# Scores and values in PSUM tiles of two banks, another order of the start-up, and twelve weight loads issued by ACT

## The chip, the cores and the metric

The kernel runs on one core of a Trainium2 chip. The metric is the device time of one execution in microseconds (us), the median over several runs. The engines are named as the profile names them: PE (TensorE, matrix multiplies), PEld (its weight loads), DVE (VectorE), ACT (ScalarE), POOL (GpSimd) and SP (SyncE, which only issues DMAs). A row with SPq or ACTq is a DMA being issued by that engine.

## What is computed

Attention over keys and values that are averaged in groups of eight, then a LayerNorm and a feed-forward block with a residual. There are 8 batches, 8 heads, 576 queries of 64 numbers a head; after the averaging 72 keys remain. All inputs and the output are float32.

```python
k_p = k.reshape(B, H, Sp, 8, D).mean(axis=3)      # 576 keys become 72
v_p = v.reshape(B, H, Sp, 8, D).mean(axis=3)
scores = scale * np.matmul(q, k_p.transpose(0, 1, 3, 2))
attn = np.exp(scores - np.max(scores, axis=-1, keepdims=True))
attn = attn / (np.sum(attn, axis=-1, keepdims=True) + 1e-09)
x = np.matmul(attn, v_p)                           # heads side by side: 4608 tokens x 512
xn = (x - mu) / np.sqrt(var + 1e-06) * g_ln
out = x + np.maximum(xn @ w_ch1, 0.0) @ w_ch2      # 512 -> 2048 -> 512
```

## The kernel before

The 4608 tokens are 36 tiles of 128; four tiles are a chunk of 512 tokens, so there are 9 chunks. A batch has 576 tokens, which is four and a half tiles, so that some tiles (4, 13, ...) hold the end of one batch and the start of the next.

*One tile of attention.* `scores` multiplies the queries `q` with the averaged keys `kblk` into PSUM (L282: 4 pairs of heads, 2 x 72 = 144 columns each, two pairs to a bank), takes the maximum over each head's 72 scores on DVE (L292, `mx`) and subtracts it (L294, `e`). A tile has two halves of four heads, each in a PSUM bank of its own, so there are two reductions of 288 columns and two subtractions. `probs` takes the exponential on ACT (L303), casts it to a high and a low float16 part (`phl`, ACT L304 and L307, POOL L311 and L314), and SP transposes it by a DMA (L321, `pt`). `values` multiplies it with the averaged values `va` and `vb` (L342, L345; 65 columns a head, the last one the sum), again in two halves of four heads in a bank each; DVE adds 1e-9 to the sums (L354, `sm`), inverts them, and DVE and ACT write the tile's `x` (L358, L365). Then comes the LayerNorm: L369 to L375, three Newton steps (L384 and L387), and `z` (L391), which is cast to two float16 parts (`hl`, ACT L395, POOL L396) and transposed by a DMA (L400, `zT`).

*The feed-forward block.* A product of floats is made of three float16 products (high by high, high by low, low by high). `ffn_in` runs 12 matmuls for 128 hidden units and a group of tokens (L419) and evicts the result with relu into a `ring` tile (ACT L427, DVE L428). `ffn_out` runs 24 matmuls for a tile and half of the hidden units (L448) and adds the result onto `x` (DVE L458). The ring has four tiles of 1 MB. For chunk 0 the columns are halved: columns 0 to 255 are tiles 0 and 1, columns 256 to 511 tiles 2 and 3.

*The weights.* `w1` and `w2` come as eight blocks of 1 MB each. `load_raw` starts the DMA of a block, `convert` turns it into float32 and finds its maxima (ACT L163 and L175, DVE L166 and L167), `max_w1` and `max_w2` find a common scale of half a matrix, and `split_w` makes the two float16 parts (ACT L138, DVE L139). The tile pool `raw` has two buffers; four blocks go to the ring, which is empty at the start.

*PSUM* has eight banks: two for `ps_s` (scores), two for `ps_x` (values) and four for `ps_f` (feed-forward).

*The order.* The string START gives, by hand, the order in which the pieces of the start-up are written: R.m.b loads block b of matrix m, C.m.b converts it, M finds a scale, S splits; A.t is scores and probabilities of tile t, B.t its values and LayerNorm; I.c.q.h is a quarter q of the hidden units of chunk c for column half h, O.c.h the output matmuls. LD is the first loads, K0 and V0 batch 0's averages, HK and HV those of later batches. Each engine runs its instructions in an order that a scheduler makes out of it; SP's queue holds the loads and transposes.

Of the kernel before, what the change touches and what calls it, by code (L numbers as in the profile page):

```python
# [17 lines left out]
P = 128  # L18
# [29 lines left out]
LD K0 R.1.0 V0 A.0 B.0 C.1.0 R.1.1 R.1.2 A.1 C.1.1 R.1.3 C.1.3 A.2 B.1 HK.1.0 C.1.2 B.2 A.3 B.3 M1.0  # L48
S.1.0 S.1.1 HK.1.1 S.1.2 S.1.3 I.0.0.1 HV.1.0 HV.1.1 A.4 I.0.1.1 R.2.0 R.2.1 I.0.1.0 I.0.0.0 A.5 B.4
B.5 A.6 R.2.2 C.2.0 R.2.3 B.6 C.2.2 C.2.1 A.7 R.1.4 C.2.3 C.1.4 B.7 M2.0 S.2.0 S.2.1 R.1.5 S.2.2  # L50
S.2.3 O.0.0 I.1.1 C.1.5 R.1.6 I.1.0 O.1.0 C.1.6 R.1.7 C.1.7 M1.1 S.1.4 S.1.5 S.1.6 S.1.7 R.2.4 R.2.5
I.0.2 R.2.6 R.2.7 HK.2.0 C.2.6 C.2.4 I.0.3 C.2.5 C.2.7 HK.2.1 HV.2.0 M2.1 S.2.4 S.2.5 A.8 S.2.6 A.9
B.8 S.2.7 HV.2.1 B.9 A.10 I.1.2 A.11 B.10 B.11 I.1.3 O.1.1 HV.3.0 O.0.1 HK.3.0 HV.3.1 HK.3.1
# [6 lines left out]
def attn_ffn_kernel(ctx: ExitStack, tc: tile.TileContext, qT, kT, v, g, w1, w2, out):  # L60
# [10 lines left out]
    ps_s = ctx.enter_context(tc.tile_pool(name="ps_s", bufs=2, space=PSUM))  # L71
    ps_x = ctx.enter_context(tc.tile_pool(name="ps_x", bufs=2, space=PSUM))
# [76 lines left out]
    def load_raw(mat, b):  # L149

        raw = ring_tile() if mat == 1 and b < NKT else raw_tile()
        raws[mat, b] = raw = raw.rearrange("p a f c -> p (a f c)").bitcast(I32)
        queue = nc.sync
        queue.dma_start(out=raw, in_=(w1, w2)[mat - 1][b].bitcast(I32))
# [117 lines left out]
    def scores(t):  # L272
# [3 lines left out]
        pss = []  # L276
        for half in range(2):
            ps = ps_s.tile([P, 512], F32, name="ps_s")
            for i in range(2):
                p = 2 * half + i  # L280
                for r, b in segments(t):
                    nc.tensor.matmul(  # L282
                        ps[r, i * 2 * KV : (i + 1) * 2 * KV],
                        lhsT=q[:, p, r],
                        rhs=kblk[b % NKB][:, p, :],
                        start=True,
                        stop=True,
                    )
            pss.append(ps[:, : 4 * KV].rearrange("p (h k) -> p h k", k=KV))
        heads = [slice(0, 4), slice(4, 8)]  # L290
        for sc, hs in zip(pss, heads):
            nc.vector.tensor_reduce(out=mx[:, hs], in_=sc, axis=AX.X, op=ALU.max)  # L292
        for sc, hs in zip(pss, heads):
# [285 lines left out]
```

## Time and profile before

| | |
|---|---|
| median of 3 runs | 913.95 us (913.83 to 914.32) |
| the profiled execution | 915.27 us; its span 913.2 us |
| PE busy | 832.8 us, 91% of the span |
| DVE busy | 440.3 us, 48% |
| ACT busy | 266.2 us, 29% |
| POOL busy | 265.1 us, 29% |
| PE's clock, mean | 0.991 of full speed |
| first 159.56 us | the start-up: tiles 0 to 7 of the attention, and of chunk 0 half of the hidden units |

A row of the timeline is: start, duration, engine, line, operation, output<-input by the program's names, shape, how often, and in brackets the idle time before it and what ended it. A row of the groups is: line, engine, operation, count | busy us, mean ns of one | idle time before, and what ended most of it. A row of the waits is: engine, tile and line <- what it waited for: us in total, times, the longest. A row of the chain is: start, us, what, and it shows the work that ended last, followed back from the last instruction. A row of stretches has for each engine the busy time and in brackets the instructions, then PE's granted clock, the DMA engines' busy share and GB/s.

### The profile page before, as it was taken

How to read it: one execution, taken by the hardware profiler on the slowest of the kernel's cores; microseconds unless marked ns; L12 is line 12 of the kernel's file. 1: busy time of each engine (PE TensorE's matmuls, PEld its weight loads, DVE VectorE, ACT ScalarE, POOL GpSimd, SP SyncE). 2: the span in 40 equal slices, each digit the busy share in tenths (PEclk: the TensorE clock that was granted, in tenths of full speed). 3: DMA queues.
4: the chain of work that ended last, by engine and by line, in shares of the span. 5: the costliest groups of instructions: out<-in, count | busy, mean ns of one | idle time of the engine just before them, and what ended most of it. 6: DMA issues, size and time to landing. Idle time of an engine off the chain costs nothing.

```text
span 913.2 us, 12100 instructions
## 1 busy us (share of the span) xinstructions
PE 832.8 (91%) x4524; PEld 418.7 (46%) x4524; DVE 440.3 (48%) x1130; ACT 266.2 (29%) x513; POOL 265.1 (29%) x414
## 2 busy tenths in 40 slices
PE   2243986999999999999999999999999999999998
PEld 1232833444444444445445544544454445444443
DVE  7797698225555445246424552554254335432121
ACT  2765563204421213132313221232223123211020
POOL 5575984005611551046101540131012001200000
PEclk9999979999999999999999999999999999999999
DMA  8999884102244322344222542232222321310001
GB/s 291 281 219 254 295 221 84 32 8 79 59 93 119 91 71 47 75 102 122 55 80 47 132 67 77 47 91 62 65 58 55 63 58 35 61 44 24 1 1 46
DMA packets 137290, 84.82 MB, mean 93 GB/s; under 512 B 116112, under 2 KB 117264, under 8 KB 135184
## 3 DMA queue, kind: packets, MB, share of 16 engines
q1 hardware_dynamic: 135696, 82.86, 35.7%
q10 hardware_dynamic: 1536, 1.20, 0.5%
q8 instruction: 35, 0.57, 0.3%
q14 instruction: 23, 0.19, 0.1%
HBM read 45.09 MB, written 9.44 MB: 60 GB/s over the span
## 4 chain that ended last, share of the span: by engine, by line
PE 82%; DMA 6%; DVE 5%; POOL 3%; issue 1%; ACT 1%; SPq 1%; ACTq 0%; POOLq 0%; DVEq 0%
PE ps_f L419 39%; PE ps_f L448 39%; PE ps_s L282 3%; DMA kr<-in_kT_dram 1%; DMA vr<-in_v_dram 1%; POOL vr L229 1%; DMA zT<-hl 1%; DMA ring<-in_w_dram 1%; PE ps_x L342 1%; DVE a L384 1%; PE ps_x L345 1%; DMA raw<-in_w_dram 1%; DMA raw<-in_v_dram 1%; DVE w L167 1%; DVE raw L166 1%
## 5 line engine op out<-in xcount | busy, mean ns | idle before, releaser
L419 PE MATMUL ps_f<-zT,w 128*128 128x512 f16 (+1 forms) x1824 | 386.3, 371 | 8.8 <-DMA zT<-hl 7.9
L448 PE MATMUL ps_f<-w,ring 128*128 128x512 f16 x1728 | 382.3, 381 | 3.4 <-DVE w L139 3.0
L419 PEld LDWEIGHTS <-w 128*128 128x128 f16 x1824 | 178.1, 99 | 198.6 <-DMA zT<-hl 7.2
L448 PEld LDWEIGHTS <-ring 128*128 128x128 f16 x1728 | 168.9, 98 | 206.1 <-issue 8.5
L428 DVE SCALAR_TENSOR_TENSOR ring<-ps_f,ring 128x512 f16<-128x512 f32 (+1 forms) x152 | 99.7, 660 | 147.2 <-ACT ring L427 144.7
L427 ACT ACTIVATE ring<-ps_f 128x512 f16<-128x512 f32 (+1 forms) x152 | 86.4, 574 | 253.4 <-PE ps_f L419 228.1
L458 DVE SCALAR_TENSOR_TENSOR x<-ps_f,c_out,x 128x512 f32<-128x512 f32 x72 | 53.9, 748 | 206.9 <-PE ps_f L448 202.5
L311 POOL TENSOR_TENSOR phl<-e,phl 128x512 f16<-128x512 f32 x36 | 43.7, 1214 | 275.2 <-ACT phl L304 260.0
L282 PE MATMUL ps_s<-kblk,q 128*128 128x144 f32 (+1 forms) x320 | 55.3, 339 | 33.5 <-DMA q<-in_qT_dram 10.7
L396 POOL TENSOR_TENSOR hl<-z,hl 128x512 f16<-128x512 f32 x36 | 42.2, 1171 | 116.0 <-ACT hl L395 110.3
L303 ACT ACTIVATE e<-e 128x576 f32<-128x576 f32 x36 | 24.6, 682 | 163.0 <-DVE e L294 138.7
L282 PEld LDWEIGHTS ps_s<-kblk,q 128*128 128x128 f32 (+1 forms) x320 | 47.6, 214 | 41.8 <-issue 25.3
L365 ACT ACTIVATE x<-ps_x,rs 128x64 f32<-128x64 f32 x144 | 33.4, 314 | 81.3 <-DVE rs L356 60.6
L229 POOL TENSOR_TENSOR vr<-vr 72x256 f32<-72x256 f32 x56 | 47.7, 858 | 24.8 <-DMA vr<-in_v_dram 24.4
L342 PE MATMUL ps_x<-va,pt 128*128 128x65 f16 (+1 forms) x320 | 28.0, 202 | 24.5 <-DVE x L358 12.6
L219 POOL TENSOR_TENSOR kblk<-kr 64x72 f32<-64x72 f32 x58 | 26.2, 452 | 72.0 <-PE ps_s L282 68.9
L304 ACT CAST phl<-e 128x1024 f16<-128x1024 f32 x36 | 37.5, 1042 | 4.6 <-DMA pt<-phl 4.0
L342 PEld LDWEIGHTS <-pt 128*128 128x128 f16 (+1 forms) x320 | 24.0, 105 | 31.2 <-issue 12.5
L395 ACT CAST hl<-z 128x512 f16<-128x512 f32 x36 | 22.2, 617 | 49.7 <-DVE z L391 49.0
L384 DVE SCALAR_TENSOR_TENSOR a<-y,ve 128x1 f32<-128x1 f32 x108 | 33.5, 310 | 2.9
L292 DVE TENSOR_REDUCE mx<-ps_s 128x4 f32<-128x288 f32 x72 | 31.6, 448 | 3.6 <-PE ps_s L282 3.3
L294 DVE TENSOR_TENSOR e<-ps_s,mx 128x288 f32<-128x288 f32 x72 | 30.7, 448 | 5.1 <-POOL phl L314 5.0
(81 smaller groups left out, 469.9 us busy)
## 6 DMA issues: line engine op xcount, KB each, us to landing
raw<-in_w_dram SPq DMA_DIRECT2D x12, 1024.0 KB
q<-in_qT_dram SPq DMA_DIRECT2D x36, 256.0 KB
out_dram<-x SPq DMA_DIRECT2D x36, 256.0 KB
kr<-in_kT_dram SPq DMA_DIRECT2D x30, 288.0 KB
vr<-in_v_dram SPq DMA_DIRECT2D x56, 144.0 KB
ring<-in_w_dram SPq DMA_DIRECT2D x4, 1024.0 KB
raw<-in_v_dram SPq DMA_DIRECT2D x8, 144.0 KB
va<-vh ACTq DMA_DIRECT2D x16, 65.0 KB
```

The source lines that it names most:

```text
L229: eng.tensor_add(out=vr[:, 0:4, :], in0=vr[:, 0:4, :], in1=vr[:, 4:8, :])
L282: nc.tensor.matmul(ps[r, i * 2 * KV : (i + 1) * 2 * KV], lhsT=q[:, p, r], rhs=kblk[b % NKB][:, p, :], start=True, stop=True,)
L304: nc.scalar.copy(out=ph[:, :, :, 0:KA], in_=e[:, :, 0:KA].unsqueeze(1).broadcast_to([P, 2, H, KA]))
L311: nc.gpsimd.tensor_tensor(out=ph[:, 0, :, KA:P], in0=e[:, :, 0:KA], in1=ph[:, 0, :, 0:KA], op=ALU.subtract)
L342: nc.tensor.matmul(px[r, i, :], lhsT=pt[:, h, r], rhs=VA[b][:, h, :], start=True, stop=False)
L384: nc.vector.scalar_tensor_tensor(out=a, in0=y, scalar=ve, in1=y, op0=ALU.mult, op1=ALU.mult)
L396: nc.gpsimd.tensor_tensor(out=zhl[:, 1, :], in0=z, in1=zhl[:, 0, :], op=ALU.subtract)
L419: nc.tensor.matmul(ps, lhsT=w[:, part, fs], rhs=zT[:, kz, cols], start=(n == 0), stop=(n == 3 * NKT - 1),)
L427: nc.scalar.activation(out=h[:, 0, i, cols], in_=ps, func=AF.Relu)
L428: nc.vector.scalar_tensor_tensor(out=h[:, 1, i, cols], in0=ps, scalar=0.0, in1=h[:, 0, i, cols], op0=ALU.max, op1=ALU.subtract,)
L448: nc.tensor.matmul(ps, lhsT=h[:, part, i, cols], rhs=w[:, wp, j], start=(n == 0), stop=(n == 3 * NFT // 2 - 1),)
L458: nc.vector.scalar_tensor_tensor(out=x, in0=ps, scalar=c_out[:, half : half + 1], in1=x, op0=ALU.mult, op1=ALU.add)
```

## The change

It has three parts. The pools `ps_s` and `ps_x` have one buffer each in place of two, and a tile of them spans two banks: a tile's eight heads lie in one PSUM tile, the maxima are one reduction of 576 columns, the subtraction is one instruction, and so is the addition to the sums. The matmuls keep their number and shapes; those of `values` now run over all eight heads for each batch in turn. START is another order. And `load_raw` issues only the first four blocks of `w1` on SP's queue, the other twelve on ACT's; the first two blocks go to `raw` tiles and two to the ring, and the first values go to the ring. Of START only the first line is shown.

```diff
-LD K0 R.1.0 V0 A.0 B.0 C.1.0 R.1.1 R.1.2 A.1 C.1.1 R.1.3 C.1.3 A.2 B.1 HK.1.0 C.1.2 B.2 A.3 B.3 M1.0
...
+LD K0 R.1.0 V0 A.0 R.1.1 B.0 A.1 R.1.2 C.1.2 C.1.0 B.1 A.2 R.1.3 C.1.1 HK.1.0 C.1.3 A.3 R.2.0 M1.0
...
-    ps_s = ctx.enter_context(tc.tile_pool(name="ps_s", bufs=2, space=PSUM))
-    ps_x = ctx.enter_context(tc.tile_pool(name="ps_x", bufs=2, space=PSUM))
+    ps_s = ctx.enter_context(tc.tile_pool(name="ps_s", bufs=1, space=PSUM))
+    ps_x = ctx.enter_context(tc.tile_pool(name="ps_x", bufs=1, space=PSUM))
...
-        raw = ring_tile() if mat == 1 and b < NKT else raw_tile()
+        early = mat == 1 and b < NKT
+        raw = ring_tile() if early and b >= 2 else raw_tile()
         raws[mat, b] = raw = raw.rearrange("p a f c -> p (a f c)").bitcast(I32)
-        queue = nc.sync
+        queue = nc.sync if early else nc.scalar
         queue.dma_start(out=raw, in_=(w1, w2)[mat - 1][b].bitcast(I32))
...
-        for half in range(2):
-            ps = ps_s.tile([P, 512], F32, name="ps_s")
...
+        ps = ps_s.tile([P, 2, 512], F32, name="ps_s")
+        for p in range(NPAIR):
+            for r, b in segments(t):
+                nc.tensor.matmul(
+                    ps[r, p // 2, p % 2 * 2 * KV : (p % 2 + 1) * 2 * KV],
...
-        for sc, hs in zip(pss, heads):
-            nc.vector.tensor_reduce(out=mx[:, hs], in_=sc, axis=AX.X, op=ALU.max)
-        for sc, hs in zip(pss, heads):
-            nc.vector.tensor_tensor(
-                out=e[:, hs, :],
...
+        nc.vector.tensor_reduce(out=mx, in_=sc, axis=AX.X, op=ALU.max)
+        nc.vector.tensor_tensor(
+            out=e.rearrange("p (a h) k -> p a h k", a=2),
+            in0=sc,
+            in1=mx.unsqueeze(3).broadcast_to([P, 2, 4, KV]),
+            op=ALU.subtract,
+        )
...
-            px = ps_x.tile([P, H // 2, D + 1], F32, name="ps_x")
...
+        ps = ps_x.tile([P, 2, 512], F32, name="ps_x")
+        px = ps[:, :, : H // 2 * (D + 1)].rearrange("p a (h d) -> p a h d", d=D + 1)
+        for r, b in segs:
+            for h in range(H):
+                o = px[r, h // 4, h % 4]
...
-        for half, px in enumerate(pxs):
-            hs = slice(half * 4, half * 4 + 4)
-            nc.vector.tensor_scalar_add(out=sm[:, hs], in0=px[:, :, D], scalar1=1e-9)
+        nc.vector.tensor_scalar_add(
+            out=sm.rearrange("p (a h) -> p a h", a=2), in0=px[:, :, :, D], scalar1=1e-9
+        )
...
-            raw_tile().rearrange("p a f c -> p (a f c)").bitcast(F32)[:KV].rearrange(
+            ring_tile().rearrange("p a f c -> p (a f c)").bitcast(F32)[:KV].rearrange(
```

What it moves in an engine's queue is shown at three places. The lines of the new kernel are lower or higher by a few: L164 and L176 are the old L163 and L175, L155 the old L154, L253 and L254 the old L252 and L253, L289 and L290 the old L292 and L294, L299 the old L303, L300 and L303 the old L304 and L307, L372 and L375 the old L384 and L387, L379 the old L391, L383 the old L395, L415 and L416 the old L427 and L428. A number behind a name is that of the tile. DMAHW names, with a number, the completion semaphore of a DMA that the instruction waits for.

ACT's queue in the first third of the start-up, before; `va` and `vb` are the values of batch 0.

```order
L163 ACTIVATE w1_88<-ring_278 128x1024 [waits DMAHW1_49]
L303 ACTIVATE e_284<-e_284 128x576 [waits DVE_49,Pool_49]
L138 ACTIVATE vh_187<-vp_152,sv_186 72x8x64 [waits DVE_49]
L304 CAST phl1_105<-e_284 128x16x64 [waits Activation_49]
L307 CAST phl1_105<-e_284 128x8x16
L163 ACTIVATE w1_88<-ring_280 128x1024 [waits DMAHW2_49]
L175 ACTIVATE ring_278,wm1_95<-w1_88 128x1024 [waits DVE_49]
L252 DMA va_188<-vh_187 64x520 [waits DMAHW6_49,Activation_49]
L253 DMA vb_189<-vh_187 8x520 [waits DMAHW7_49]
```

The same place after; raw_406 and raw_435 are the first two blocks of `w2`, and e_273 is tile 1.

```order
L164 ACTIVATE w1_88<-raw_219 128x1024 [waits DMAHW1_49]
L155 DMA raw_406<-in_w2_dram 128x2048 [waits DMAHW4_49,Activation_49]
L299 ACTIVATE e_273<-e_273 128x576 [waits DVE_49]
L300 CAST phl1_105<-e_273 128x16x64 [waits Activation_49]
L303 CAST phl1_105<-e_273 128x8x16
L176 ACTIVATE raw_219,wm1_95<-w1_88 128x1024 [waits DVE_49]
L138 ACTIVATE vh_187<-vp_152,sv_186 72x8x64 [waits DVE_49]
L164 ACTIVATE w1_88<-ring_289 128x1024 [waits DMAHW2_49]
L155 DMA raw_435<-in_w2_dram 128x2048 [waits DMAHW5_49,Activation_49]
L253 DMA va_188<-vh_187 64x520 [waits DMAHW6_49,Activation_49]
L254 DMA vb_189<-vh_187 8x520 [waits DMAHW7_49]
```

Two loads now stand between the conversions, one ahead of tile 1's exponential and one ahead of `va`, each with a wait for an earlier DMA's semaphore of its own.

ACT's queue where batch 1's `va` and `vb` are issued, before.

```order
L427 ACTIVATE ring_559<-ps_f_605 128x256 [waits PE_49]
L138 ACTIVATE vh_671<-vp_622,sv_670 72x8x64 [waits DMAHW0_49,DVE_49]
L252 DMA va_672<-vh_671 64x520 [waits DMAHW7_49,Activation_49]
L253 DMA vb_673<-vh_671 8x520 [waits DMAHW0_49]
L252 DMA va_672<-vh_671 64x520 [waits DMAHW2_49]
L253 DMA vb_673<-vh_671 8x520 [waits DMAHW4_49]
L427 ACTIVATE ring_710<-ps_f_711 128x256 [waits PE_49]
```

The same place after; raw_1083 is a block of `w1`, z_503 and z_552 are tiles 2 and 3, and e_1035 is tile 7.

```order
L155 DMA raw_1083<-in_w1_dram 128x2048 [waits DMAHW2_49,Activation_49]
L299 ACTIVATE e_1035<-e_1035 128x576 [waits DVE_49]
L138 ACTIVATE vh_588<-vp_441,sv_587 72x8x64 [waits DVE_49]
L253 DMA va_589<-vh_588 64x520 [waits Activation_49]
L383 CAST hl_505<-z_503 128x512 [waits DMAHW7_49,DVE_49]
L254 DMA vb_590<-vh_588 8x520
L253 DMA va_589<-vh_588 64x520 [waits DMAHW0_49]
L254 DMA vb_590<-vh_588 8x520 [waits DMAHW2_49]
L383 CAST hl_554<-z_552 128x512 [waits DVE_49]
L415 ACTIVATE ring_652<-ps_f_653 128x256 [waits PE_49]
L415 ACTIVATE ring_652<-ps_f_668 128x256 [waits PE_49]
```

The `va` and `vb` stood between evictions of chunk 0 (L427), and the tiles' casts were done; now they stand ahead of the first eviction, and the casts of tiles 2 and 3 stand between and behind them.

DVE's queue before, around tile 3's `z` (z_518).

```order
L387 SCALAR_TENSOR_TENSOR y_508<-a_509,y_508 128x1
L384 SCALAR_TENSOR_TENSOR a_509<-y_508,ve_507 128x1
L387 SCALAR_TENSOR_TENSOR y_508<-a_509,y_508 128x1
L391 TENSOR_SCALAR z_518<-x_475,mv2_504,y_508 128x512
L294 TENSOR_TENSOR e_1128<-ps_s_1130,mx_1129 128x288
L294 TENSOR_TENSOR e_1128<-ps_s_1133,mx_1129 128x288
L166 TENSOR_SCALAR raw_1147<-raw_1147 128x1024
```

DVE's queue after, from tile 7's subtraction (e_1035) to tile 2's `z` (z_503).

```order
L290 TENSOR_TENSOR e_1035<-ps_s_1037,mx_1036 128x576
L372 SCALAR_TENSOR_TENSOR a_494<-y_493,ve_492 128x1
L363 TENSOR_SCALAR y_542<-ve_541 128x1
L133 TENSOR_REDUCE allmax_581<-ps_f_584 128x1
L167 TENSOR_SCALAR raw_1077<-raw_1077 128x1024
L375 SCALAR_TENSOR_TENSOR y_493<-a_494,y_493 128x1
L372 SCALAR_TENSOR_TENSOR a_543<-y_542,ve_541 128x1
L111 TENSOR_SCALAR sv_587<-allmax_581 128x1
L250 TENSOR_SCALAR cv_594<-allmax_581 128x1
L168 SCALAR_TENSOR_TENSOR w1_88<-w1_88,raw_1077 128x1024
L379 TENSOR_SCALAR z_503<-x_462,mv2_489,y_493 128x512
```

Tile 7's subtraction, one instruction of 576 columns, stood behind tile 3's `z` (there as e_1128 in two halves) and stands now ahead of the `z` of tiles 2 and 3.

58 lines of the change are left out of this document (18 added, 40 removed).

## The prediction

> **What bounds the kernel now.** I read the stretches first, cut where PE's state changes: the fourth score tile's LayerNorm, the first FFN matmul, the first output matmul, the first matmul of chunk 1.
>
> ```profile
> core 0: us, PE busy (x) PEld busy (x) DVE busy (x) ACT busy (x) POOL busy (x), PEclk, DMA share, GB/s
> 0.00:79.26 79.26, 25.84 (x154) 20.28 (x154) 65.65 (x169) 41.48 (x70) 50.16 (x83) 1.00 0.95 256
> 79.26:154.15 74.89, 57.43 (x394) 37.41 (x394) 58.88 (x130) 40.14 (x74) 54.98 (x76) 0.93 0.81 227
> 120.58:159.56 38.98, 29.92 (x161) 14.65 (x161) 35.68 (x86) 16.99 (x32) 25.34 (x32) 0.85 0.59 135
> 159.56:913.20 753.64, 747.30 (x3968) 359.08 (x3968) 312.44 (x821) 182.03 (x365) 157.72 (x254) 1.00 0.26 63
> ```
>
> From 159.56 on PE is busy 747.30 of 753.64 us, and the change leaves its matmuls as they are; whatever DVE, ACT or POOL save there is covered by PE, and what remains is 6.3 us of gaps. Before 159.56 PE has much idle time, DVE little: 65.65 of 79.26 and 58.88 of 74.89. So the change can pay, or cost, in the start-up, and the question is when PE starts chunk 1. Next, PE's timeline at the ends of its gaps:
>
> ```profile
> 88.81 8.02 PE L419 MATMUL ps_f<-zT,w 128*128 128x256 f16 x48 [6.82 <-DMA zT<-hl]
> 159.56 22.29 PE L419 MATMUL ps_f<-zT,w 128*128 128x512 f16 x96 [1.04 <-DMA zT<-hl]
> 204.87 1.32 PE L282 MATMUL ps_s<-kblk,q 128*64 128x144 f32 x16 [1.21 <-issue]
> 218.99 10.52 PE L419 MATMUL ps_f<-zT,w 128*128 128x512 f16 x48 [0.77 <-DVE ring L428]
> ```
>
> Both starts of the FFN end on a transpose zT. The chain of waits says what stands ahead of each:
>
> ```profile
> 50.98 7.85 DMA raw<-in_w_dram
> 58.86 2.27 DVE raw L166
> 78.71 0.55 DVE z L391
> 82.96 5.80 DMA zT<-hl
> 129.98 0.68 DVE mv L235
> 153.60 0.55 DVE z L391
> 156.05 3.37 DMA zT<-hl
> ```
>
> In the chain DVE's own work runs with few breaks from 58.83, where the weight block lands, to tile 3's z (79.26), and from about 130 to tile 7's z (154.15); chunk 1 then starts 5.4 us later. Ahead of 58.83 it is a load. I therefore count DVE's queue up to these two places, and ask what interrupts it.
>
> **The change part by part.** *Merged PSUM tiles.* The rows of the old shapes, grouped by form over the first 165 us, and one pair in place:
>
> ```profile
> 81.83 0.82 DVE L292 TENSOR_REDUCE mx<-ps_s 128x4 f32<-128x288 f32 x2
> L428 DVE SCALAR_TENSOR_TENSOR ring<-ps_f,ring 128x256 f16<-128x256 f32 x16 | 6.4, 419 | 6.4 <-ACT ring L427 6.2
> L428 DVE SCALAR_TENSOR_TENSOR ring<-ps_f,ring 128x512 f16<-128x512 f32 x1 | 0.7, 691 | 3.6 <-ACT ring L427 3.6
> L354 DVE TENSOR_SCALAR sm<-ps_x 128x4 f32<-128x4 f32 x18 | 2.3, 148 | 0.6 <-PE ps_x L345 0.6
> ```
>
> No 576-wide score operation exists before. From 256 to 512 elements the PSUM-reading L428 grows by 272 ns, 1.06 ns an element; 576 would be 0.691 + 64 x 1.06 = 0.76 us, an estimate. Two halves back to back take 0.82, so each merged operation saves 0.06; its bounds are 0.69 (the 512-wide one) and 0.82 (no gain). Of the two sm additions one goes: 0.15 a tile. After the start-up all of it lies under PE.
>
> *One buffer instead of two.* PE may now write a tile's scores only when DVE has subtracted the last tile's.
>
> ```profile
> PE ps_s L282 <- DVE e L294: 2.9, 2, 1.7
> PE ps_x L342 <- DVE x L358: 12.6, 4, 4.8
> ```
>
> PE waited 2.9 us in two cases for the scores' buffers and 12.6 in four for the values' in 0 to 165, with two half tiles to spare. In the new order the FFN's first 68 matmuls stand in PE's queue behind the scores of tile 8, and these wait for DVE's subtraction of tile 7's: that subtraction is the new gate, the place that tile 3's z had. It is counted below. Elsewhere PE has idle time in the start-up, and I take nothing: between 0 and 4.8, the longest single wait.
>
> *The order.* Chunk 0's FFN begins with columns 0 to 255, which need tiles 0 and 1, where before it began with 256 to 511 (tiles 2 and 3). So tile 2's and 3's LayerNorm tails leave the stretch ahead of the gate and come behind it; two more weight conversions come ahead. DVE's rows in question:
>
> ```profile
> L167 DVE SCALAR_TENSOR_TENSOR w<-w,raw 128x1024 int32<-128x1024 int32 x12 | 16.9, 1405 | 2.4 <-ACT w L163 2.2
> L166 DVE TENSOR_SCALAR raw<-raw 128x1024 int32<-128x1024 int32 x12 | 10.5, 876 | 4.1 <-DMA raw<-in_w_dram 4.1
> L384 DVE SCALAR_TENSOR_TENSOR a<-y,ve 128x1 f32<-128x1 f32 x24 | 13.2, 550 | 0.4
> L387 DVE SCALAR_TENSOR_TENSOR y<-a,y 128x1 f32<-128x1 f32 x24 | 4.9, 204 | 0.3
> L391 DVE TENSOR_SCALAR z<-x,mv,y 128x512 f32<-128x512 f32 x8 | 5.4, 676 | 0.3
> L458 DVE SCALAR_TENSOR_TENSOR x<-ps_f,c_out,x 128x512 f32<-128x512 f32 x4 | 2.9, 730 | 0.0
> ```
>
> Ahead of the gate, counted in both programs: conversions 8 to 10, +2 x (0.876 + 1.405) = +4.56; Newton steps 12 to 8, -4 x (0.550 + 0.204) = -3.02; z 4 to 2, -2 x 0.676 = -1.35; scores 15 pairs to 16 merged, 16 x 0.76 - 15 x 0.82 = -0.14; four sm, -0.59. Sum -0.5, so the gate falls at 79.26 - 0.5 = 78.8 if nothing else moves. From the gate to tile 7's z: conversions 8 to 6, -4.56; Newton steps 12 to 16 and z 4 to 6, +4.37; one output eviction fewer, -0.73; scores 5 pairs to 4 merged, 4 x 0.76 - 5 x 0.82 = -1.06; four sm, -0.59. Sum -2.6: DVE has 58.88 - 2.6 = 56.3 us of work.
>
> What matters more is DVE's idle time in that stretch, 74.89 - 58.88 = 16.0:
>
> ```profile
> DVE ring L428 <- ACT ring L427: 6.2, 4, 2.5
> DVE raw L166 <- DMA raw<-in_w_dram: 3.1, 3, 1.5
> DVE w L167 <- ACT w L163: 1.7, 4, 0.5
> DVE e L294 <- POOL phl L314: 1.7, 1, 1.7
> ```
>
> Before, DVE had little but conversions to do while the first FFN matmuls waited 6.82 us for zT, and then waited for evictions. Now the FFN can start right at the gate, because the zT it needs was begun 24 DVE instructions earlier, and the z of tiles 2 and 3 stand between the evictions. Of 16.0 I let the loads' 3.1 and POOL's 1.7 go, and half of the 6.2; 8.1 is left. It may be as low as 3 (little but ACT's 1.7 and scraps stay) or stay at 16. PE's own work there is no bound: 57.43 us from about 81 would be done by 139.
>
> *Loads issued by ACT.* Twelve 1 MB loads leave SP's queue. What they did there, and what ACT's own DMAs did to ACT:
>
> ```profile
> 50.98 0.90 SPq L154 DMA_DIRECT2D raw<-in_w_dram  x2
> 51.99 9.39 SPq L321 DMA_TRANSPOSE pt<-phl  x1
> 159.92 1.76 SPq L321 DMA_TRANSPOSE pt<-phl  x1
> 32.68 1.12 ACT L163 ACTIVATE w<-ring 128x1024 f32<-128x1024 f32 x1 [4.27 <-DMA vr<-in_v_dram]
> 101.09 0.94 ACT L427 ACTIVATE ring<-ps_f 128x256 f16<-128x256 f32 x3 [3.01 <-DMA vb<-vh]
> 71.23 0.42 SPq L154 DMA_DIRECT2D raw<-in_w_dram  x1
> 79.45 1.16 ACT L163 ACTIVATE w<-raw 128x1024 f32<-128x1024 f32 x1 [2.89 <-DMA raw<-in_w_dram]
> ```
>
> A load takes its issuer about 0.45 us: 12 x 0.45 = 5.4 us leave SP and come to ACT, which is busy 41.48 of 79.26 us and has room. But each DMA, of either queue, uses one of eight completion semaphores in turn, and its issuer waits until the DMA eight before it has landed. SP had nothing to do behind such a wait but more DMAs; behind ACT's load of the first block of w2 stands an exponential, and behind batch 1's va and vb stand a cast hl and the first FFN evictions. Before, such a wait held ACT 4.27 us (va, vb of batch 0) and 3.01 (batch 1). Two new stalls come ahead of the gate, before the exponentials of tiles 1 and 2; each lies between 0 and 4.27, and part of it takes the place of the old 4.27, since the same queue reaches va and vb later. I take 2.5 in all, from 0 to 5.
>
> The Trainium skill, page "DMA: Bandwidth & Descriptors", section "Anatomy of one DMA — SWDGE (gpsimd) path", says that DMA engines do not wait on semaphores and that any such wait is on the sequencer which issues. By that rule the trace agrees: ACT's 4.27 us stood at its own DMAs, with nothing of ACT running.
>
> *Sum.* Gate 78.8 + 2.5 = 81.3; + 56.3 + 8.1 = 145.7 for tile 7's z; + 5.4 = 151.1 for chunk 1 against 159.56: -8.5. Behind it, the maxima of w1's second half stand ahead of chunk 1's output matmuls in the new order, so the 1.21 at 204.87 should go: -1.2 (0 to -2.0 with the 0.77). Total -9.7. The profiled execution, 913.2 of span and 2.07 around it, is 915.27, 1.3 above the median 913.95; from the median the forecast is 904.2, said as 904.
>
> **Rivals.** *Slower: ACT as issuer.* In the new program vb of batch 1 waits for the landing of a 1 MB load issued just before it. The rows at 71.23 and 79.45 show such a landing: 8.2 us from issue to use. For that time ACT would hold the cast for tile 3 and four evictions, PE would fill its four ps_f banks and stop, and DVE would wait for ACT as in its 6.2 us row. If this 8.2 falls on the path whole, the stalls ahead of the gate reach 5 (+2.5), and one later load holds ACT for 3.01, it gives 904.2 + 13.7 = 918. It decides once the stalls beyond my 2.5 pass 11.6 us. For it speaks that ACT's rows show such stalls in every batch; against it that ACT is idle half the stretch (40.14 of 74.89) and DVE has 56 us of its own to go on with. 0.21.
>
> *No change: the DMA engines bound the start.* Their share is 0.95 up to 79.26 and 0.81 after, and the chain passes 7.85 us of a weight load at 50.98. The bytes are the same. If all landings keep their time, the gate moves by little and the new order gains only what PE loses later: 913.95 - 1.2 = 912.8. Against it speaks that the share falls to 0.59 from 120.58 on, while DVE is busy 35.68 of 38.98 there: the end of the start-up is DVE's. 0.13.
>
> The Trainium skill, same page, section "Issuing engines are not separate DMA queues", holds that DMAs of several issuers run on the same engines and that a second issuer saves only the sequencer's time. By that rule moving the loads is worth nothing on this path, and the time would be this rival's. The trace does not settle it: a transpose behind two loads took 9.39 us and alone 1.76, which is what shared engines and a shared queue would both give.
>
> *More: transposes freed.* If pt's 9.39 came from standing behind SP's own weight loads, it becomes about 1.76 and the values of two tiles come 7.6 us earlier, ahead of the gate: 904.2 - 7.6 = 897. It needs DVE to have work ready then; its 13.6 idle us before 79.26 are the most that can go. 0.16.
>
> **How the numbers follow.** The forecast (899 to 911) has 0.50. About 0.2%, 1.8 us, is what a measurement can tell from none. Faster is forecast and freed transposes, 0.66; same 0.13; slower 0.21. Lower end: idle 3 (-5.1), no stall (-2.5), gaps -0.8 and part of the freed transposes: 893. Upper end: idle 16 (+7.9) and stalls 5 (+2.5) give 914.6; the slower rival's lower half reaches 917, with some 0.15 left out in all.
>
> **What would show it.** Right: chunk 1's first 96-matmul block starts near 151; the first FFN matmul near 82, right behind the scores of tile 8; DVE idle near 8 us between; no gap at 205; PE full after. Wrong: ACT idle before L299 or L383 for more than 3 us behind its own DMA rows; DVE's wait for ACT's evictions above 6.2; transposes pt still 9 us long with no load on SP's queue (then the engines are shared and the load's queue meant nothing); new waits of scores or values for DVE in 160 to 913, where I count none.

## The result, and the profile after

The changed kernel is slower: 927.76 us in the median of 20 executions (916.05 to 949.05), against 914.69 for the kernel before (912.03 to 917.07, 20 executions). The ratio of comparable executions is 1.0095, 95% interval 1.0071 to 1.0118. It leaves out executions over 1.5% above the kernel's fastest, and since this kernel alone spreads over 33 us, that cuts into its own spread; in a second series the median was 931.03 (922.64 to 938.09), ratio 1.0142 [1.0106, 1.0177]. Spread is the first finding: 5 us before, 33 after. Both profiles of the changed kernel (934.01 and 935.26 us) come from executions slower than its median, so that a typical one may lose less at the places shown.

Forecast were 904 us, a range of 893 to 917, and 0.21 for slower. Stretches of the second profile of the changed kernel (span 933.5), in the columns of the prediction; the last row is the kernel before:

```profile
core 0: us, PE busy (x) PEld busy (x) DVE busy (x) ACT busy (x) POOL busy (x), PEclk, DMA share, GB/s
0.00:80.00 80.00, 22.48 (x130) 17.57 (x130) 57.61 (x113) 38.99 (x62) 49.08 (x82) 1.00 0.96 243
80.00:160.00 80.00, 41.96 (x330) 31.99 (x331) 43.73 (x121) 35.58 (x70) 32.75 (x47) 0.89 1.11 182
200.00:930.00 730.00, 729.29 (x3891) 351.68 (x3889) 312.25 (x739) 174.97 (x356) 152.50 (x250) 1.00 0.25 63
```

```profile
80.00:160.00 80.00, 59.85 (x404) 39.24 (x404) 61.58 (x140) 42.13 (x78) 57.54 (x79) 0.91 0.77 214
```

From 200 us on PE is full, as before. The loss is in the start-up, and there every engine works less than before: DVE 43.73 of 80 us in the second stretch, against 61.58. Only the DMA engines are busier (a share of 1.11 against 0.77; it adds up the times of single packets), and they move less (182 GB/s against 214). PE's timeline, the chain of waits and a row of SP's queue of the same execution:

```profile
105.27 5.84 PE L407 MATMUL ps_f<-zT,w 128*128 128x256 f16 x48
133.01 5.09 PE L407 MATMUL ps_f<-zT,w 128*128 128x256 f16 x28 [12.96 <-DMA zT<-hl]
183.11 20.89 PE L407 MATMUL ps_f<-zT,w 128*128 128x512 f16 x96 [0.20 <-DMA zT<-hl]
```

```profile
24.25 22.11 DMA pt<-phl
83.39 20.96 DMA raw<-in_w_dram
115.95 25.51 DMA pt<-phl
```

```profile
115.95 21.25 SPq L317 DMA_TRANSPOSE pt<-phl  x1
```

The first FFN matmul comes at 105.27 (before: 88.81) and chunk 1 at 183.11 (before: 159.56). Three DMAs of 20 to 26 us stand on the chain, two transposes and a weight load; before the change the longest DMA on the chain took 11.07. SP was busy issuing the last transpose for 21.25 us, and its next DMA went out at 137.29. The longest one before:

```profile
20.86 11.07 DMA vr<-in_v_dram
```

In the first profile of the changed kernel (934.01 us) they are nearly the same ones, and a whole row of engines waits for the last:

```profile
25.78 19.00 DMA pt<-phl
82.12 16.93 DMA raw<-in_w_dram
111.77 26.55 DMA pt<-phl
```

```profile
138.34 1.04 ACT L300 CAST phl<-e 128x1024 f16<-128x1024 f32 x1 [17.10 <-DMA pt<-phl]
139.90 0.42 DVE L416 SCALAR_TENSOR_TENSOR ring<-ps_f,ring 128x256 f16<-128x256 f32 x1 [16.17 <-ACT ring L415]
140.38 5.53 PE L407 MATMUL ps_f<-zT,w 128*128 128x256 f16 x26 [14.57 <-DVE ring L416]
```

ACT stands at its cast into `phl`, whose last reader, the transpose, has not landed; the FFN's evictions are behind that cast in ACT's queue, DVE waits for ACT, and PE for DVE. In the second profile the weights are as late: in the first 200 us DVE waits 32.1 us for blocks of `raw` to land (before: 4.1).

### The profile page after: what moved, and what is told of

Same layout as the page of the kernel before. It is cut to its first block, busy times and chain, and to the rows that moved or that the text cites. A ratio compares the mean times of both kernels' runs of the same rounds, so it can differ in the third digit from the quotient of the medians.

```text
span 932.2 us, 11952 instructions
## 1 busy us (share of the span) xinstructions
PE 831.9 (89%) x4524; PEld 420.6 (45%) x4524; DVE 438.6 (47%) x1022; ACT 263.6 (28%) x513; POOL 259.9 (28%) x414
## 4 chain that ended last, share of the span: by engine, by line
PE 78%; DMA 11%; DVE 5%; POOL 2%; ACT 1%; issue 1%; SPq 0%; ACTq 0%; POOLq 0%
PE ps_f L407 37%; PE ps_f L436 36%; DMA pt<-phl 5%; PE ps_s L280 3%; DMA raw<-in_w_dram 2%; DMA kr<-in_kT_dram 2%; PE ps_x L336 1%; PE ps_x L337 1%; DVE w L168 1%; DMA ring<-in_v_dram 1%; DVE a L372 1%; DVE w L139 1%; POOL kr L216 1%; POOL phl L307 0%; DVE y L375 0%
## 5 line engine op out<-in xcount | busy, mean ns | idle before, releaser
L407 PE MATMUL ps_f<-zT,w 128*128 128x512 f16 (+1 forms) x1824 | 390.4, 374 | 21.6 <-DVE ring L416 15.6
L407 PEld LDWEIGHTS <-w 128*128 128x128 f16 x1824 | 180.3, 100 | 213.5 <-issue 21.6
L416 DVE SCALAR_TENSOR_TENSOR ring<-ps_f,ring 128x512 f16<-128x512 f32 (+1 forms) x152 | 99.7, 659 | 157.5 <-ACT ring L415 156.3
L415 ACT ACTIVATE ring<-ps_f 128x512 f16<-128x512 f32 (+1 forms) x152 | 86.7, 574 | 259.2 <-PE ps_f L407 241.4
L307 POOL TENSOR_TENSOR phl<-e,phl 128x512 f16<-128x512 f32 x36 | 42.5, 1180 | 287.5 <-ACT phl L300 273.9
L384 POOL TENSOR_TENSOR hl<-z,hl 128x512 f16<-128x512 f32 x36 | 42.7, 1186 | 115.8 <-ACT hl L383 113.8
L299 ACT ACTIVATE e<-e 128x576 f32<-128x576 f32 x36 | 24.6, 682 | 171.9 <-DVE e L290 158.4
L230 POOL TENSOR_TENSOR vr<-vr 72x256 f32<-72x256 f32 x56 | 43.2, 775 | 23.8 <-DMA vr<-in_v_dram 22.1
L300 ACT CAST phl<-e 128x1024 f16<-128x1024 f32 x36 | 37.5, 1041 | 26.2 <-DMA pt<-phl 25.6
L383 ACT CAST hl<-z 128x512 f16<-128x512 f32 x36 | 22.2, 617 | 65.7 <-DVE z L379 57.2
L232 POOL TENSOR_TENSOR vp<-vr 72x64 f32<-72x64 f32 x56 | 20.3, 373 | 59.1 <-DVE vb L139 58.8
L357 DVE BATCH_NORM_STATS2 st<-x 128x6 f32<-128x512 f32 x36 | 24.8, 690 | 23.1 <-ACT x L353 23.0
L372 DVE SCALAR_TENSOR_TENSOR a<-y,ve 128x1 f32<-128x1 f32 x108 | 31.8, 295 | 2.8
```

The costliest lines, as they stand in the source:

```text
L230: eng.tensor_add(out=vr[:, 0:4, :], in0=vr[:, 0:4, :], in1=vr[:, 4:8, :])
L300: nc.scalar.copy(out=ph[:, :, :, 0:KA], in_=e[:, :, 0:KA].unsqueeze(1).broadcast_to([P, 2, H, KA]))
L307: nc.gpsimd.tensor_tensor(out=ph[:, 0, :, KA:P], in0=e[:, :, 0:KA], in1=ph[:, 0, :, 0:KA], op=ALU.subtract)
L372: nc.vector.scalar_tensor_tensor(out=a, in0=y, scalar=ve, in1=y, op0=ALU.mult, op1=ALU.mult)
L384: nc.gpsimd.tensor_tensor(out=zhl[:, 1, :], in0=z, in1=zhl[:, 0, :], op=ALU.subtract)
L407: nc.tensor.matmul(ps, lhsT=w[:, part, fs], rhs=zT[:, kz, cols], start=(n == 0), stop=(n == 3 * NKT - 1),)
```

## The experiments

Theory A: transposes on SP's queue and 1 MB loads on ACT's meet in the DMA engines, and both get slow. Theory B, the slower rival of the prediction: ACT is held at its loads. C: the order. D: the single PSUM buffers. All times are medians, with the lowest and highest execution. The runs were made in four series; the kernel before has medians of 914.37 to 915.47 in them, so that a difference of 1 us between two series says nothing.

**The changed kernel again.** No edit.

> The changed kernel once more, for a second profile and beside the others on one chip. Every theory: median near 926, runs spread over more than 15 us, since what differs from run to run would be the timing of DMAs against each other. In the profile, transposes (pt, zT) that meet weight loads of ACT's queue land late (20 us and more) in this execution too, but perhaps others of them than in the first profile.

931.03 us (922.64 to 938.09), 5 above the expected 926; the chain above is this one. The wide spread and the late transposes came, and they are nearly the same transposes as in the first profile.

**The loads back on SP.**

```diff
-        queue = nc.sync if early else nc.scalar
+        queue = nc.sync
```

> The changed kernel with all sixteen weight loads on SP's queue; order and PSUM tiles as changed. Theory A (a transpose on one queue beside weight loads on another is slowed down by them): the time falls to 905 to 915 and the spread to some 5 us, no transpose lands later than 12 us after its issue. Theory B (ACT is held at its loads): the same fall, but the transposes stay as long as before the change, 9 to 13 us. Theory C (the new order is what costs): stays above 920. Theory D (single PSUM buffers): stays above 920.

906.58 us (905.14 to 908.39), ratio 0.9909 [0.9888, 0.9931]: 24.5 us less than the same kernel with ACT's queue in the same series (21.2 less than its first 20 executions), and a spread of 3. C and D fall as the cause of the loss. The longest transpose on the chain takes 9.02 us, within A's 12. The profile, at the places of the prediction:

```profile
24.69 9.02 DMA pt<-phl
```

```profile
83.68 8.13 PE L407 MATMUL ps_f<-zT,w 128*128 128x256 f16 x48
142.99 0.21 PE L336 MATMUL ps_x<-va,pt 128*128 128x65 f16 x1 [7.23 <-DVE z L379]
154.41 22.41 PE L407 MATMUL ps_f<-zT,w 128*128 128x512 f16 x96 [0.80 <-DMA zT<-hl]
```

The same 20 us in both kernels, loads on ACT first, loads on SP second:

```profile
84.00:104.00 20.00, 2.11 (x20) 1.87 (x21) 6.04 (x20) 4.29 (x9) 2.81 (x3) 1.00 1.08 115
```

```profile
84.00:104.00 20.00, 20.00 (x170) 16.87 (x169) 15.89 (x33) 13.26 (x27) 14.81 (x23) 1.00 1.02 282
```

The engines' share is over 1 in both; with two queues they move 115 GB/s, with one 282. The two stretches hold different DMAs (transposes and weights in the first; also q, k and v in the second), but packets of the same size differ too: one of a transpose (256 bytes) takes 97 ns on average in the first and 28 in the second, one of a weight load (8 KB) 716 and 361. At the times that the quick packets need (18 ns and 309), the packets of the first stretch would fill about a third of it, an estimate from these traces.

Counted over the first 200 us of each profile, as the packets of the trace have it (a load's packets are 8 KB, 8128 bytes with the slices and in the mirror below, partly 4 KB in the halves):

| kernel | us | transposes' packets: mean ns | those over 100 ns | loads' packets over 2 us |
|---|---|---|---|---|
| before | 915 | 25 | 169 | 1 |
| loads on SP | 907 | 24 | 233 | 0 |
| changed, first profile | 928 | 37 | 1167 | 55 |
| changed, second profile | 931 | 38 | 1171 | 60 |
| ACT's loads on the old order | 921 | 23 | 210 | 1 |
| slices | 912 | 22 | 161 | 0 |
| halves | 914 | 34 | 1500 | 3 |
| mirror | 922 | 26 | 437 | 8 |

The lower rows belong to runs that follow. The slow packets of the transposes do not go with the time. The loads' packets of over 2 us, up to 10, are many only in the changed kernel's two profiles of this table, and there they lie around the chain's three long DMAs (in the second profile 18, 26 and 16 of the 60).

**PSUM tiles alone**, on the old order with the old queue (the diff's hunks for `ps_s`, `ps_x`, `scores` and `values`).

> The kernel before with PSUM tiles of two banks, one buffer each, as the only change. Theories A, B, C: within 2 us of before, at best 1 us faster from the shorter DVE work in the start-up. Theory D: 3 us or more slower, with PE waiting for L290 or L346 in the start-up.

916.20 us (913.66 to 918.17), ratio 1.0014 [1.0000, 1.0027]. A cost of about 1 us, by the interval 2.5 at most: not D at 3 us, and no gain.

**The order alone** (START, the first blocks' places; loads on SP, old PSUM tiles).

> The kernel before with the new order and the new places of the first loads, all loads on SP, PSUM tiles as before. My sum gave the order itself about -8 us: theories A and B 903 to 914. Theory C: above 920.

902.07 us (901.24 to 902.61), ratio 0.9858 [0.9840, 0.9877]: 13 us faster, and 1 below the expected range.

```profile
80.14 7.67 PE L420 MATMUL ps_f<-zT,w 128*128 128x256 f16 x48
151.73 21.51 PE L420 MATMUL ps_f<-zT,w 128*128 128x512 f16 x96 [0.51 <-DMA zT<-hl]
```

7.8 us come ahead of chunk 1 (159.56 to 151.73) and 5.9 behind it: 899.5 - 151.73 = 747.8 against 753.64. Of the 5.9, 3.6 are work of PE that now stands ahead of chunk 1 (743.75 us busy behind it against 747.30), and 2.3 are gaps.

**ACT's loads alone**, on the old order and PSUM tiles.

```diff
-        queue = nc.sync
+        queue = nc.sync if mat == 1 and b < NKT else nc.scalar
```

> The kernel before with its twelve later weight loads issued by ACT, as the only change (old order, old PSUM tiles). On the changed order this queue cost 24.5 us (931.0 against 906.6). Theory A (transposes on one queue and 1 MB loads on another slow each other down) and theory B (ACT is held at its loads) both: 10 to 30 us slower than before, 925 to 945, with a spread of 10 us or more. Theory A's mark: a transpose that lands over 15 us after its issue. If it stays within 3 us of before, the cost belongs to the new order and the queue together.

920.94 us (919.37 to 924.73), ratio 1.0070 [1.0052, 1.0088]: slower by 6, less than either theory had. On the old order the same move costs a quarter of the 24.5, so that most of that belongs to the queue and the new order together. The profile shows no long transpose here (23 ns a packet), so A's mark is missing. It shows a load at the head of ACT's queue that waits, with the first exponential behind it:

```profile
22.18 1.28 ACT L303 ACT_TABLE_LOAD   x1 [22.18 <-DMA ring<-in_w_dram]
```

The exponential starts at 23.47 in place of 18.13. But the first transposes, which come after it, are issued at 28.17 (before: 28.21), so this wait is not shown to cost anything. Where the 6 us come from stays open.

**Small DMAs on ACT in the loads' place.** At each late load, which SP issues, ACT issues 64 bytes to a small tile.

```diff
-        queue = nc.sync if early else nc.scalar
+        queue = nc.sync
...
+        if not early:
+            nudge = wk2.tile([4, NKT], F32, name="nudge")
+            nc.scalar.dma_start(out=nudge, in_=g[0:4, :])
```

> The changed kernel with all weight loads on SP, as in the run before this one that did 906.6; at each place where ACT would issue a load it issues a DMA of 64 bytes to a small tile instead. ACT keeps its waits for completion semaphores and its issue time; the bulk is on one queue. Theory A: 905 to 910. Theory B: 920 or more.

916.78 us (915.02 to 921.36). The test was badly made: the small DMAs depend on nothing, so all twelve stand at the head of ACT's queue, and ACT does nothing until 13.43 us. It shows what twelve idle DMAs ahead of the work cost, not theory B at the loads' places.

**Slices on ACT.** SP issues the late blocks but for the last 64 bytes of each row, which ACT issues into the same tile.

```diff
-        queue = nc.sync if early else nc.scalar
-        queue.dma_start(out=raw, in_=(w1, w2)[mat - 1][b].bitcast(I32))
+        block = (w1, w2)[mat - 1][b].bitcast(I32)
+        n = block.shape[-1] if early else block.shape[-1] - 16
+        nc.sync.dma_start(out=raw[:, :n], in_=block[:, :n])
+        if not early:
+            nc.scalar.dma_start(out=raw[:, n:], in_=block[:, n:])
```

> Loads on SP as in the run that did 906.6, but the last 64 bytes of each row of the twelve later blocks are issued by ACT as a DMA of their own (8 KB in all for a block). They go to the same tile as the block, so ACT issues them at the place, and with the waits, that the changed kernel's loads had; the nudges of the earlier run could all go to the head of ACT's queue and told nothing of this. Theory B (ACT is held at its loads): 920 or more. Theory A (the bulk on a second queue): 905 to 912. In between, say 915, both matter in about equal parts.

912.49 us (911.17 to 914.86): 5.9 more than with the loads on SP alone, and just above A's 905 to 912. I count it as B's share, with all that twelve more DMAs and another order of the scheduler's bring. The wait at batch 1's `va` and `vb`, for which I had feared 8.2 us, took 5:

```profile
94.16 0.94 ACT L418 ACTIVATE ring<-ps_f 128x256 f16<-128x256 f32 x3 [5.01 <-DMA va<-vh]
```

**The mirror: bulk on ACT, slices on SP** (n = 16 in the diff above). Both queues have as many DMAs as with the slices, only the bytes change sides; the scheduler moves some instructions between the two.

> The mirror of the slices kernel: SP issues the first 64 bytes of each row of the twelve blocks, ACT the rest. Both queues have the same number of DMAs as in the slices kernel; only the bytes change sides. Theory A: 925 to 937, spread 10 us or more, transposes that take 20 us. Theory B: 911 to 915.

922.31 us (920.05 to 925.14): 9.8 more than the slices, nearer to A's range than to B's but under it. A's other signs did not come: the spread is 5, and the longest transpose takes SP 11.3 us to issue. SP's queue and PE's timeline; the row behind them is the slices':

```profile
24.08 15.90 SPq L320 DMA_TRANSPOSE pt<-phl  x2
166.08 23.44 PE L410 MATMUL ps_f<-zT,w 128*128 128x512 f16 x96 [4.94 <-DMA zT<-hl]
```

```profile
25.00 7.96 SPq L320 DMA_TRANSPOSE pt<-phl  x2
```

The first two transposes take 15.90 us to issue, 7.96 with the slices. That is the main place where the mirror's transposes are slow; over 200 us their packets take 26 ns on average, about as before. So the bytes' change of side costs, but only a part of it is shown to go through slow transposes.

**Halves** (n = half a row).

> As the slices kernel (912.5), but ACT issues the second half of each row (512 KB of each of the twelve blocks) and SP the first half. ACT has the same number of DMAs, at the places and with the waits of the slices. If the bulk on the second queue is what costs (theory A), the time lies between 912.5 and 931, near 920, with a spread of 8 us or more. If the waits of ACT cost (theory B), it stays at 911 to 914.

914.10 us (911.61 to 920.70): 1.6 above the slices, spread 9. The spread is A's; the time is nearer to B's. Its profile has more slow packets of transposes (1500, 34 ns on average) than the changed kernel's, so slow transposes alone need not cost: it depends on whether the chain runs through them. The effect is not in proportion to the bytes.

**Everything on ACT's queue**, the transposes too.

```diff
-        nc.sync.dma_start_transpose(out=PT[t], in_=ph.rearrange("p a h k -> p (a h k)"))
+        nc.scalar.dma_start_transpose(out=PT[t], in_=ph.rearrange("p a h k -> p (a h k)"))
...
-        nc.sync.dma_start_transpose(
+        nc.scalar.dma_start_transpose(
```

> The changed kernel with the transposes too on ACT's queue, so that weight loads and transposes are in one queue, and ACT waits more than before: for POOL ahead of each transpose, and for semaphores. Only loads of q, k and v and the output stay on SP. Theory A: transposes no longer run beside 8 KB packets of weights, and in spite of ACT's longer waits the time falls below 925, with transposes that land within 13 us. Theory B: 935 or more. A result between them would say that both matter.

923.01 us (915.28 to 926.07): 8 less than the changed kernel in the second series, 5 less than in the first, although ACT now also waits for POOL ahead of each transpose. The time is under A's 925, but A's other sign, transposes that land within 13 us, did not come: one took 16.53 on the chain, beside SP's loads of q, k and v. The run does not decide between the theories.

```profile
97.05 16.53 DMA pt<-phl
```

**DMAs alone, three kernels.** Rounds of transposes (of pt's size, SP) and 1 MB loads, a DVE instruction between rounds that waits for all of them. The rows are DVE's; the bracket is the wait for the round.

> No attention and no feed-forward: only DMAs in rounds that a DVE instruction separates, each twice. Two transposes of the size of pt on SP alone; two 1 MB loads on ACT alone; both at once; all four on SP, loads first; all four on SP, transposes first; transposes on SP and the loads in 2 KB rows on ACT; loads on SP and transposes on ACT. Output is not the attention's. Theory A: alone about 4 us a pair of transposes and 6 to 8 us a pair of loads; on one queue about their sum, 10 to 13 us; on two queues clearly more than the sum, 15 to 25 us. Theory B: on two queues no more than the sum. With 2 KB rows, if the engines alternate packet by packet, less loss a packet but more packets.

```profile
20.59 0.16 DVE L80 TENSOR_TENSOR src<-pt,pt 128x1 f16<-128x1 f16 x1 [6.95 <-DMA pt<-src]
28.31 0.16 DVE L83 TENSOR_TENSOR src<-raw,raw 128x1 f16<-128x1 f32 x1 [7.36 <-DMA raw<-in_kT_dram]
41.08 0.16 DVE L80 TENSOR_TENSOR src<-pt,pt 128x1 f16<-128x1 f16 x1 [12.61 <-DMA pt<-src]
53.67 0.16 DVE L80 TENSOR_TENSOR src<-pt,pt 128x1 f16<-128x1 f16 x1 [12.29 <-DMA pt<-src]
60.87 0.16 DVE L80 TENSOR_TENSOR src<-pt,pt 128x1 f16<-128x1 f16 x1 [6.90 <-DMA pt<-src]
```

Two transposes 6.95 us, two loads 7.36, both at once on two queues 12.61, on one queue with the loads first 12.29; with the transposes first these land after 6.90 and the loads 6.07 later. No loss on two queues here, against A's 15 to 25; but transposes that are first on one queue land in 6.9 us and beside a second queue in 12.6. Loads in rows of 2 KB gave 15.69, and loads on SP with transposes on ACT 12.24. In the second pass each round came within 1 us of the first.

> DMAs alone again, in rounds, each twice, now staggered, since in the earlier rounds the loads were nearly through when the transposes began to move. Four transposes of pt's size on SP alone (about 13 us by the earlier rounds); the same with two 1 MB loads on SP; the same with two loads on ACT that start some 4 us later; four loads on ACT with the transposes 2 us behind; transposes and four loads of 288 KB mixed on SP with two late loads on ACT; four loads of 288 KB, then transposes, with loads on ACT at once. The output is not the attention's. If what slowed the transposes in the changed kernel (packets of 256 bytes took 100 to 200 ns in place of 20, for 20 us) is a matter of two queues alone, one of these rounds shows it: 40 us or more where the sum is 20 to 25. If all rounds end at their sum, the two queues only share, and the long stretches need something else that the kernel has and this has not.

```profile
39.62 0.23 DVE L88 TENSOR_TENSOR src<-pt,pt 128x1 f16<-128x1 f16 x2 [11.99 <-DMA pt<-src]
58.63 0.16 DVE L88 TENSOR_TENSOR src<-raw,raw 128x1 f16<-128x1 f32 x1 [2.76 <-DMA raw<-in_kT_dram]
82.09 0.23 DVE L88 TENSOR_TENSOR src<-pt,pt 128x1 f16<-128x1 f16 x2 [23.17 <-DMA pt<-src]
132.95 0.16 DVE L88 TENSOR_TENSOR src<-pt,pt 128x1 f16<-128x1 f16 x1 [28.09 <-DMA pt<-src]
```

Four transposes 12.0; with two loads on the same queue 18.4 (15.17 for the transposes, and the loads by 58.63); with two loads on ACT that come in while the transposes run 23.2, and the transposes are last. With loads of 288 KB mixed in on SP 28.1, where the parts sum to some 24 (12.0, 7.4, and 1.15 MB at the loads' rate, 4.2). Where the loads came first, two queues took less than the sum: 21.5 for 27, and 19 for 24 with loads of 288 KB ahead of the transposes. So a load from the second queue that meets running transposes loses 4 to 5 us in 19; the 40 us did not come. The packets show the same split. In the four rounds (two kinds, both passes) in which loads come in on ACT while the transposes run, 5, 11, 12 and 8 packets of loads took over 2 us, and the transposes' packets 30 to 39 ns on average; in the other eight rounds no packet took over 2 us, and that average was 20 to 22. So the changed kernel's long load packets come with DMAs alone too, where two queues meet in this way. The 100 to 200 ns that the expectation gives for a transpose's packet in the changed kernel are too high as a mean: it is 97 over the 20 us from 84 us.

> DMAs alone: two transposes of pt's size on SP and one 1 MB load. First with the load on SP behind them, then with the load on ACT, started after 0 to 6 ACT copies of about 1 us, each three times. Two transposes alone took 7.0 us in the earlier rounds, two loads 7.4. If a load that meets transposes under way is what costs, delay 0 ends near the sum of 11 us, delays of 2 to 4 us some 2 to 10 us above it, and a delay of 6 near the sum again. If all delays end within 1 us of the one-queue round, the loss is not in this pair alone. The output is not the attention's.

```profile
20.92 0.16 DVE L84 TENSOR_TENSOR src<-pt,pt 128x1 f16<-128x1 f16 x1 [9.94 <-DMA pt<-src]
52.95 0.16 DVE L84 TENSOR_TENSOR src<-pt,pt 128x1 f16<-128x1 f16 x1 [10.72 <-DMA pt<-src]
66.55 0.16 DVE L84 TENSOR_TENSOR src<-pt,pt 128x1 f16<-128x1 f16 x1 [13.20 <-DMA pt<-src]
74.04 0.16 DVE L84 TENSOR_TENSOR src<-pt,pt 128x1 f16<-128x1 f16 x1 [7.10 <-DMA pt<-src]
```

Two transposes and one load: one queue 9.94; on ACT 9.7 to 10.9 with delays of 0 to 2 us; with 3 us 13.20, then 12.73, then 10.48 in the three repetitions; with 4 us the transposes are through first (7.05 to 8.06). The loss depends on the moment, and at the same moment it comes or not.

**Which PSUM tile costs.** On the order alone, first the scores' tile of two banks, then the values'.

> The order-only kernel (902.1) with the scores' PSUM tile of two banks and one buffer; values as before. The full PSUM change cost 4.5 us on this order. If PE must wait for the scores' subtraction (the single ps_s buffer), this kernel has most of it: 905 to 908. If it is the values' buffer: 901 to 903.

900.93 us (899.59 to 902.13), ratio 0.9848 [0.9829, 0.9867]: no cost, and perhaps 1 us less than the order alone (the ranges overlap). Its median is the lowest here.

> The order-only kernel with the values' PSUM tile of two banks and one buffer; scores as before. If the single ps_x buffer is what costs: 905 to 908; if the scores' buffer: 901 to 903. If neither alone gives 3 us, the two act together or the instructions' new order does it.

905.45 us over six executions, one of which took 1796.69; the other five are 901.87 to 907.64, median 904.59. By that 2.5 of the 4.5 us are the values' tile, but the range touches that of the order alone (901.24 to 902.61).

## Why the prediction was wrong

In terms of the sum, with the runs in the order of the steps:

| step | forecast us | measured us |
|---|---|---|
| order (from the sum: DVE's work -0.7, its idle time -7.9, the gap at 205 -1.2) | -9.8 | -13.0 (902.07 against 915.11) |
| scores' tile, on the new order | -1.2 | -1.1, within the ranges |
| both PSUM tiles, on the new order | -2.4 (DVE's shorter work) | +4.5 (906.58 against 902.07) |
| ACT's issue and waits | +2.5 | +5.9 (912.49 against 906.58) |
| bulk on the second queue | 0, or a gain | +9.8 (922.31 against 912.49) |
| not assigned | | +8.7 (931.03 against 922.31; +5.5 with the first series' 927.76) |

**What bounds the kernel** was right: the start-up, and PE full behind it; the gap at 205 is gone. That the change leaves PE's work behind chunk 1 as it is was not quite right (3.6 us of it moved ahead with the new order). The gain of the rest of the change was right in its sign: without the term for ACT my sum gives 904.2 - 2.5 = 901.7, and with the loads on SP it measured 906.6, a gain of 8.5 in place of 12.2. Chunk 1 started at 154.41, where the sum without that term says 148.6; the first FFN matmul at 83.68, for "near 82". That it came so near was in part luck, since two errors offset each other: the order gave 13.0 where the sum has 9.8, and the PSUM tiles cost 4.5 where the sum lets them save 2.4, with the single buffer priced at nothing between bounds of 0 and 4.8. A place where that may happen is the row at 142.99: PE waits 7.23 us ahead of its values' matmuls, released by a `z` in DVE's queue; that this wait is the buffer's and not the order's is argued, not shown.

**The step that failed** is the term "loads issued by ACT", 2.5 us from 0 to 5, which measured 24.5 (21.2 with the first series). I bounded it by the rows of ACT's own stalls, 4.27 and 3.01. These are stalls of the issuer, and for the issuer the size was of the right kind, 5.9 by the slices. What I did not price is what the loads do to other DMAs: I took the transpose that stood 9.39 us behind two loads (a row of SP's issuing, not of the landing) as a cost that ends when the loads leave the queue, and gave a gain from it 0.16. The opposite came: beside a second queue the transposes landed later than behind the loads, up to 26.55 us, and the loads landed late too, up to 20.96. The queue of SP had been an order, in which a transpose that was ahead of a load kept its place (6.90 us in the rounds of DMAs alone, 12.61 beside a second queue). The Trainium skill, page "DMA: Bandwidth & Descriptors", section "Queues, rings and completion order", has the rule that I did not weigh: each DMA engine takes turns between the queues it has work for, a packet at a time. The packets of the trace agree: where 8 KB packets of another queue are about (309 ns each when quick), 70 and 72% of the slow transposes' packets (in the two profiles) took 300 to 360 or 600 to 670 ns, the time of one or two of them; with 4 KB packets (159 ns) in the halves, three quarters took 150 to 200 or 300 to 360. Whether the page's packet is the trace's, no run shows. Taking turns would shift time from one queue to the other; it does not account for the time that two queues lost together (23.2 us against 18.4 in the staggered rounds). With that loss go load packets that stood for 2 to 10 us, in the changed kernel as in those rounds, and why they stand is open.

Of the signs of being wrong that the prediction names, three came in the changed kernel: ACT idle for 3.91 and 4.10 us (in the first and the second profile) ahead of an exponential, L299, that stands behind its first load; transposes `pt` still long without loads on SP's queue; and, in the first profile only, DVE's wait for ACT's evictions, 16.9 us between 80 and 165 (4.1 in the second).

**The rivals.** The slower one came by its sign and near its 918, but its mechanism, ACT held at its loads, carries 5.9 of 24.5; its place, batch 1's `vb`, cost 5.0 there. The DMA-bound rival had the right resource with the wrong reason: not bytes, since these are the same, but that the engines moved them more slowly. The sentence of the Trainium skill, page "DMA: Bandwidth & Descriptors", section "Issuing engines are not separate DMA queues", that DMAs of several issuers run on the same engines and interleave, agrees with these traces: from 84 to 104 us the packets of SP's and ACT's queues have shares of 0.58 and 0.50 of the same engines. The 912.8 that I drew from it did not come, since two queues had a price of their own: 23.2 against 18.4 us in the staggered rounds.

**What stays open.** The 8.7 us between the changed kernel and the mirror: the bulk is on ACT in both, but the scheduler's order differs somewhat, and only the changed kernel's profiles have 20 us stretches of slow packets on the chain, with 55 and 60 packets of loads over 2 us against the mirror's 8. Spread over 16 engines these make 18 and 22 us an engine, an estimate that lies near the loss. The staggered rounds bring such packets with DMAs alone, 5 to 12 in a round, but what holds one is not known. Why such a stretch lasts 20 us with one or two loads in it, where DMAs alone lost 5 at most, is not settled either, nor why the old order lost 6 us without it. And the scheduler plans anew for each of these kernels, so each difference holds some of that.

## What to carry to other kernels

A queue is also a priority: if small, urgent DMAs (transposes) and large loads share the DMA engines, moving the loads to another queue takes from the urgent ones the place that the order had given them. Here that cost 21 to 25 us on one order of the start-up and 6 on another. Before such a move, look for rows in which a transpose and a load are under way together, and take it that the transpose lands when the load does, not when it would alone. Test the parts of a change apart: here the order alone is 1.4% faster than before, and the queue hid it.

## What the hardware showed that I had not expected

The DMA engines' busy share did not tell what they moved: 1.08 at 115 GB/s and 1.02 at 282 in the same 20 us of two kernels, since a packet's time includes its waiting. Transposes' packets of 256 bytes took 22 ns on average alone, and 97 in such a stretch beside 8 KB packets of another queue; most kept 18 ns, and one in six took over 100, mostly the time of one or two whole packets of the other queue. The loss depended on the moment (13.20, 12.73 and 10.48 us for the same round). The changed kernel's time spread over 33 us, where the kernels with one queue for both mostly spread over 1 to 5.
